# Loads in order of use, products in runs by kind, and scores and comparisons moved in a recurrent attention kernel with a routed block

## The chip, the cores and the metric

One core of one Trainium2 chip runs the kernel. Its engines are TensorE (PE, whose weight loads the profile lists as PEld), VectorE (DVE), ScalarE (ACT), GpSimd (POOL) and SyncE (SP), which issues DMAs here. The metric is the device time of one execution in microseconds (us): the median of the runs.

## What is computed

The first part is a recurrence over 768 steps, for 4 batches of 8 heads of width 48:

```python
for t in range(S):
    cur = np.einsum('bhd,bhe->bhde', u[None] * kt, vt)
    y[:, :, t] = np.einsum('bhd,bhde->bhe', rt, state + cur)
    state = wt[:, :, :, None] * state + np.einsum('bhd,bhe->bhde', kt, vt)
```

The heads are laid side by side to rows `x` of 384. The second part scores each row against `w_gate`, takes in each batch the 128 rows with the highest scores, and adds to these rows what two matrices (384 x 1024 and 1024 x 384, with a relu between) make of them, times the sigmoid of the score. The other rows pass through:

```python
scores = np.einsum('bsd,d->bs', x, w_gate)
for b in range(B):
    top_idx = np.argpartition(-scores[b], capacity)[:capacity]
    xe = x[b, top_idx]
    ye = np.maximum(xe @ w1, 0.0) @ w2
    out[b, top_idx] = xe + g[:, None] * ye
```

## The kernel before, in words

The sequence is cut into 24 chunks of 128 rows, six in each batch, and the recurrence is turned into matrix products within a chunk and a state of 48 x 48 for each head, carried from chunk to chunk. All is float32. Heads stand in pairs, one head in the lower and one in the upper 64 partitions, so that four pairs make tiles of 128 x 512.

One chunk goes through these steps. Four loads bring `w`, `k`, `r` and `v` (L120 to L128), in runs of 48 numbers. `decays_t` (L202) transposes `w` on PE to PSUM. `scans` (L206) multiplies it up from both ends on DVE, two scans of 511 numbers. `scaled` (L239) transposes `k` and `r` on PE and multiplies them with the scans on DVE: K and R. `own_products` (L245) makes r k u on POOL; `own_values` (L251) sums it on DVE ("own") and multiplies `v` with the sum on POOL (`vo`). `scores` (L259) multiplies K and R on PE; `masked` (L269) takes the lower triangle on DVE, in two operations of 512. `back` (L275) transposes K back on PE and copies it on ACT (`kt`). `outputs_t` (L282) makes the chunk's output on PE: for each pair of heads first products of `v` and the masked scores (L290, all 128 rows of the array), then, if there is an old state, products of the state and R (L298, 64 rows each), added in the same PSUM bank. ACT copies the result; `rows_out` (L305) transposes it, adds `vo` on DVE to `x` and stores `x`. `row_scores` (L315) multiplies `x` with `w_gate` and sums, one operation on DVE. `carry_products` (L323) and `carry` (L335) make the new state on PE, DVE and POOL. `range_check` (L230) sums on ACT what of `w` lies out of its range; a general path behind the main one is taken only if there is any.

When all six chunks of a batch have scores, `mixture(b)` (L353) runs: the scores are spread over 128 x 768 by PE transposes and ACT copies (`every`), six DVE operations compare each chunk's scores with all that do not lie ahead of it (L380), 21 small products and two DVE operations make ranks, `pick` marks who has which rank, products make the row numbers, an indirect DMA of POOL gathers the rows (`xe`), PE transposes them, and DVE and ACT make the gate. It is a generator: each `yield` ends a piece. `forward` (L464) is a second one, with eight pieces of hidden products (six matrix products in each, two hidden halves that ACT copies out with a relu) and eight of last products; at its end the rows are scattered back.

The order of the work is written out by hand: `turn(i)` (L528) lists the steps, for chunks i-1 to i+2 at once, and under `manual_schedule` each engine keeps that order. A turn calls `mix` twice, one piece of the mixture each, and `fed` twice, for one and two pieces of the forward (`PIECES` is 3). A mixture starts two turns after its batch's last chunk was begun and takes twelve pieces, six turns. Turns go from -2 to 24; then a tail (L559 to L567) runs the last mixture and the last two forwards.

Buffers set further limits. `w`, `k` and `r` have four each, `v` five. PSUM has eight banks: one for `w`, two for all other transposes and small results (psT), two for the scores, and one each for output (psY), state (psK) and forward (psM). `load(i + 5)` at the end of turn i brings all four inputs of chunk i+5 into the buffers of chunk i+1 (`v`: of chunk i). `load(3)` stands both ahead of the turns (L137) and in turn -2 (L551). Both weight matrices are loaded at the end of turn 0, in two DMAs of 1.5 MB. All of these DMAs, and the stores of `x`, are issued by SP in that order.

Of the kernel before, what the change touches and what calls it, by code (L numbers as in the profile page):

```python
# [38 lines left out]
def kernel(  # L39
# [80 lines left out]
    def load(n):  # L120
        if n >= N:
            return
        b, ci = chunks[n]
        for bufs, x in ((w_bufs, w), (k_bufs, k), (r_bufs, r), (v_bufs, v)):
# [5 lines left out]
    load(0)  # L130
    u_bc = consts.tile([L, H, D], FP32)
    nc.sync.dma_start(out=u_bc, in_=_rows(u, L))
    load(1)
    wg_bc = consts.tile([L, C], FP32)
    nc.sync.dma_start(out=wg_bc, in_=_rows(moe_w_gate, L))
    load(2)
    load(3)  # L137
    w1 = consts.tile([L, NDC, F], FP32)
    w2 = consts.tile([L, NFC, C], FP32)

    def load_weights():
        nc.sync.dma_start(out=w1, in_=moe_w1.rearrange("(n p) f -> p n f", p=L))
        nc.sync.dma_start(out=w2, in_=moe_w2.rearrange("(n p) c -> p n c", p=L))


    ident = consts.tile([L, L], FP32)
# [19 lines left out]
    behind = consts.tile([L, S], FP32)  # L166
    nc.gpsimd.memset(behind[:, L:S], 1.0)
    nc.vector.tensor_copy(out=behind[:, 0:L], in_=before_f)
# [100 lines left out]
    def masked(t):  # L269
        ps = t.pop("ps_s")  # L270
        t["sc"] = lev.tile([L, 2, HP, L], FP32, tag="sc", name="sc")
        for par in (0, 1):
            nc.vector.tensor_mul(t["sc"][:, par], ps[:, par], _heads(before_f, HP))  # L273

    def back(t):  # L275
        ps = transposed(psT, "t", lambda j: t["K"][:, j, :])
# [5 lines left out]
    def outputs_t(t):  # L282

        n = t["n"]
        vt = v_bufs[n % VBUF]
        old = state.get(n)
        ps = psY.tile([L, HP, L], FP32, tag="y", name="ps_yt")
        for j in range(HP):
            for par in (0, 1):
                nc.tensor.matmul(  # L290
                    ps[DP * par:DP * par + DP, j, :], vt[:, 2 * j + par, :],
                    t["sc"][:, par, j, :], start=True, stop=(old is None),
                )
            if old is None:
                continue
            for par in (0, 1):
                rows = slice(DP * par, DP * par + DP)
                nc.tensor.matmul(  # L298
                    ps[DP * par:DP * par + D, j, :], old[rows, j, :], t["R"][rows, j, :],
                    start=False, stop=True,  # L300
                )
        t["yt"] = lev.tile([L, HP, L], FP32, tag="yt", name="yt")
        nc.scalar.copy(out=t["yt"], in_=ps)  # L303
# [11 lines left out]
    def row_scores(t):  # L315
        b, ci = chunks[t["n"]]
        scr = lev.tile([L, C], FP32, tag="scr", name="scr")
        nc.vector.tensor_tensor_reduce(
            out=scr, in0=t.pop("x"), in1=wg_bc, scale=1.0, scalar=0.0, op0=ALU.mult,
            op1=ALU.add, accum_out=score[:, b, ci:ci + 1],  # L320
        )

    def carry_products(t):  # L323
# [26 lines left out]

    groups = [(c0, min(L, CAP - c0)) for c0 in range(0, CAP, L)]

    def mixture(b):  # L353


        every = mod.tile([L, S], FP32, name="every")
        for hf in range(2):
            ps = psT.tile([L, NHF, L], FP32, tag="t", name="ps_e")
            for q in range(NHF):
                c = hf * NHF + q  # L360
                nc.tensor.transpose(  # L361
                    ps[:, q, :], score[:, b, c:c + 1].to_broadcast([L, L]), ident
                )
            nc.scalar.copy(
                out=every[:, hf * NHF * L:(hf + 1) * NHF * L],
                in_=ps.rearrange("p q t -> p (q t)"),
            )
        yield


        ahead = mod.tile([L, NCH, S], BF16, name="ahead")
        won = mod.tile([L, NCH], FP32, name="won", bufs=2)
        for cs in ((0,), (1, 2), range(3, NCH)):
            if 0 not in cs:
                yield
            for c in cs:
                if c >= NCH:
                    continue
                lo = c * L
                nc.vector.scalar_tensor_tensor(  # L380
                    out=ahead[:, c, lo:S], in0=every[:, lo:S], scalar=score[:, b, c:c + 1],
                    in1=behind[:, 0:S - lo], op0=ALU.is_le, op1=ALU.mult,
                    accum_out=won[:, c:c + 1],
                )
            yield
# [12 lines left out]
        for gi, (c0, n) in enumerate(groups):
# [65 lines left out]
    def forward(b, n, rows, where, xe, xeT, gate):  # L464

        hid = mod.tile([L, NFC, L], FP32, name="hid")
        for f0 in range(0, NFC, 4):
            ps = psM.tile([L, 4, L], FP32, tag="m", name="ps_h")
# [25 lines left out]
        yield  # L494
# [73 lines left out]


    def general(gen):  # L570
        u_t = gen.tile([D, H], FP32, name="u_t")
        nc.sync.dma_start(out=u_t, in_=u.rearrange("h d -> d h"))
        for b in range(B):
# [27 lines left out]
            for c in range(NCH):  # L601
                x = lev.tile([L, C], FP32, tag="x", name="x", bufs=3)
                nc.sync.dma_start(out=x, in_=out[b, c * L:(c + 1) * L, :])
                scr = lev.tile([L, C], FP32, tag="scr", name="scr")
                nc.vector.tensor_tensor_reduce(
                    out=scr, in0=x, in1=wg_bc, scale=1.0, scalar=0.0,
                    op0=ALU.mult, op1=ALU.add, accum_out=score[:, b, c:c + 1],
                )
# [41 lines left out]
```

## Time and profile before

| | us |
|---|---|
| median of 3 runs | 272.96 |
| lowest and highest | 271.13, 276.75 |
| the profiled execution | 272.69 |
| its span, first to last instruction | 270.9 |
| PE busy, DVE busy | 230.1, 211.8 |
| POOL busy, ACT busy | 98.9, 77.0 |

The profile shows one execution. Times of rows count from the start of the span. A line of a timeline gives start, duration, engine, line, operation, output and inputs, the number of instructions merged (a matrix product in float32 counts twice) and in brackets how long the engine sat idle before, and what ended that. Ends of matrix products are modelled, so the start of the next instruction is the safer mark. In a row of windows, each engine's busy time (and count) stands in the order PE, PEld, DVE, ACT, POOL, then the granted share of PE's clock, the DMA share and GB/s.

### The profile page before, as it was taken

Reading aid. Unit: us, or ns where it says so; the run is one execution under the profiler, and the core shown is the slowest. Engines: PE = TensorE matmul, PEld = TensorE weight load, DVE = VectorE, ACT = ScalarE, POOL = GpSimd, SP = SyncE. Lnnn points to the kernel's source line nnn. Section 1 sums busy time; section 2 is a strip of 40 time slices with the busy share of each in tenths; the row PEclk is TensorE's granted clock in tenths of the full one; section 3 lists DMA queues with packets and bytes.
Section 4 is the critical chain, followed back from the end, with each engine's and each line's share of the span. In section 5 each row is a group of like instructions: output and inputs, shape, how many; then the busy total and the mean of one; then the engine's idle time right before and its main releaser. Section 6 shows DMA issues by size and latency. Waiting matters only on the chain.

```text
span 270.9 us, 5843 instructions
## 1 busy us (share of the span) xinstructions
PE 230.1 (85%) x2290; PEld 169.9 (63%) x2290; DVE 211.8 (78%) x431; ACT 77.0 (28%) x201; POOL 98.9 (37%) x108
## 2 busy tenths in 40 slices
PE   3783999999798699795999899994999899989780
PEld 2572677776665467674688476584778566685740
DVE  6894478999999998999999999789889994373010
ACT  5450203333442121344323213233213301220100
POOL 3243405554433550844055326334236331102000
PEclk9998569999999858999999999999899999999997
DMA  9999999999996363488545635944000000201001
GB/s 129 180 176 166 162 285 327 179 191 205 193 173 115 67 114 87 92 171 119 111 76 109 127 75 96 171 108 72 31 30 2 29 31 23 68 29 29 31 0 42
DMA packets 109732, 29.96 MB, mean 111 GB/s; under 512 B 104576, under 2 KB 108928, under 8 KB 109696
## 3 DMA queue, kind: packets, MB, share of 16 engines
q1 hardware_dynamic: 109184, 27.93, 58.2%
q0 software_dynamic: 512, 1.57, 1.8%
q8 instruction: 20, 0.33, 0.6%
q14 instruction: 16, 0.13, 0.2%
HBM read 23.99 MB, written 5.51 MB: 109 GB/s over the span
## 4 chain that ended last, share of the span: by engine, by line
PE 44%; DVE 7%; ACT 4%; issue 1%; POOL 0%; ACTq 0%
PE ps_h L471 9%; PE ps_f L481 8%; PE ps_yt L290 6%; PE ps_yt L298 6%; PE ps_t L199 5%; PE ps_s L264 4%; PE ps_kv L330 2%; ACT kt L278 1%; ACT hid L476 1%; PE ps_w L199 1%; DVE left L224 1%; PE ps_e L361 1%; DVE right_buf L212 1%; DVE scr L444 1%; PE ps_y L199 1%
## 5 line engine op out<-in xcount | busy, mean ns | idle before, releaser
L255 POOL TENSOR_TENSOR vo<-v_buf,own 128x384 f32<-128x384 f32 x24 | 25.2, 1051 | 106.5 <-DVE own L253 102.4
L290 PE MATMUL ps_yt<-sc,v_buf 128*64 128x128 f32 x384 | 41.8, 309 | 4.0 <-DVE x L309 4.0
L303 ACT COPY yt<-ps_yt 128x512 f32<-128x512 f32 x24 | 14.1, 586 | 106.9 <-PE ps_yt L298 99.0
L273 DVE TENSOR_TENSOR sc<-ps_s,before_f 128x512 f32<-128x512 f32 x48 | 30.8, 682 | 12.4 <-PE ps_s L264 12.4
L298 PE MATMUL ps_yt<-R,state 64*48 64x128 f32 x320 | 35.7, 302 | 0.0
L290 PEld LDWEIGHTS ps_yt<-sc,v_buf 128*64 128x64 f32 x384 | 20.1, 141 | 21.2 <-issue 14.1
L212 DVE TENSOR_TENSOR_SCAN right_buf<-ps_w,from_right 128x511 f32<-128x511 f32 x24 | 29.0, 1210 | 5.3 <-PE ps_w L199 5.3
L248 POOL TENSOR_TENSOR rk<-r_buf,k_buf 128x384 f32<-128x384 f32 x24 | 30.9, 1289 | 4.0 <-DMA r_buf<-in_r_dram 4.0
L224 DVE TENSOR_TENSOR_SCAN left<-ps_w,from_left 128x511 f32<-128x511 f32 x24 | 30.7, 1280 | 0.9
L264 PE MATMUL ps_s<-R,K 48*128 48x128 f32 x384 | 30.6, 304 | 0.0
L264 PEld LDWEIGHTS ps_s<-R,K 48*128 48x128 f32 x384 | 25.7, 204 | 4.6 <-issue 2.3
L471 PE MATMUL ps_h<-xeT,w 128*128 128x128 f32 x192 | 25.5, 283 | 2.0 <-ACT hid L476 1.4
L380 DVE SCALAR_TENSOR_TENSOR ahead<-every,score,behind 128x768 bf16<-128x768 f32 (+5 forms) x24 | 27.0, 1165 | 0.1
L481 PE MATMUL ps_f<-w,hid 128*128 128x384 f32 x64 | 24.3, 506 | 2.2 <-ACT hid L476 2.2
L249 POOL TENSOR_TENSOR rk<-rk,u_bc 128x384 f32<-128x384 f32 x24 | 25.3, 1053 | 2.6 <-DMA u_bc<-in_u_dram 0.8
L199 PE MATMUL ps_w<-ident,w_buf 128*128 128x128 f32 x96 | 16.5, 301 | 10.1 <-DVE slots L162 4.2
L471 PEld LDWEIGHTS ps_h<-xeT,w 128*128 128x128 f32 x192 | 23.1, 195 | 3.0 <-ACT hid L476 1.8
L298 PEld LDWEIGHTS ps_yt<-R,state 64*48 64x48 f32 x320 | 14.0, 123 | 15.2 <-issue 14.8
L278 ACT COPY kt<-ps_t 128x512 f32<-128x512 f32 x24 | 14.0, 585 | 30.3 <-PE ps_t L199 30.1
L199 PE MATMUL ps_t<-ident,r_buf 128*128 128x128 f32 x96 | 16.5, 298 | 3.7 <-ACT kt L278 2.3
L243 DVE TENSOR_TENSOR R<-ps_t,left 128x512 f32<-128x512 f32 x24 | 16.4, 684 | 3.9 <-PE ps_t L199 2.0
L199 PEld LDWEIGHTS ps_w<-ident,w_buf 128*128 128x128 f32 x96 | 12.7, 157 | 10.7 <-issue 10.7
(89 smaller groups left out, 326.1 us busy)
## 6 DMA issues: line engine op xcount, KB each, us to landing
w_buf<-in_w_dram SPq DMA_DIRECT2D x25, 192.0 KB, 4.1
k_buf<-in_k_dram SPq DMA_DIRECT2D x25, 192.0 KB, 4.8
r_buf<-in_r_dram SPq DMA_DIRECT2D x25, 192.0 KB, 5.0
v_buf<-in_v_dram SPq DMA_DIRECT2D x25, 192.0 KB, 4.3
out_dram<-x SPq DMA_DIRECT2D x24, 192.0 KB, 2.1
w<-in_moe_w_dram SPq DMA_DIRECT2D x2, 1536.0 KB, 9.7
u_bc<-in_u_dram SPq DMA_DIRECT2D x1, 192.0 KB, 4.6
wg_bc<-in_moe_w_gate_dram SPq DMA_DIRECT2D x1, 192.0 KB, 5.2
```

The source lines that it names most:

```text
L199: nc.tensor.transpose(ps[:, j, :], src(j), ident)
L212: nc.vector.tensor_tensor_scan(out=flat[:, W - 2::-1], data0=wt[:, W - 1:0:-1], data1=from_right.rearrange("p j t -> p (j t)")[:, W - 2::- ...
L224: nc.vector.tensor_tensor_scan(out=left.rearrange("p j t -> p (j t)")[:, 1:W], data0=wt[:, 0:W - 1], data1=start.rearrange("p j t -> p (j ...
L248: nc.gpsimd.tensor_mul(rk, r_bufs[n % NBUF][:, :, 0:D], k_bufs[n % NBUF][:, :, 0:D])
L249: nc.gpsimd.tensor_mul(rk, rk, u_bc)
L264: nc.tensor.matmul(ps[:, par, j, :], t["K"][rows, j, :], t["R"][rows, j, :], start=True, stop=True,)
L273: nc.vector.tensor_mul(t["sc"][:, par], ps[:, par], _heads(before_f, HP))
L290: nc.tensor.matmul(ps[DP * par:DP * par + DP, j, :], vt[:, 2 * j + par, :], t["sc"][:, par, j, :], start=True, stop=(old is None),)
L298: nc.tensor.matmul(ps[DP * par:DP * par + D, j, :], old[rows, j, :], t["R"][rows, j, :], start=False, stop=True,)
L380: nc.vector.scalar_tensor_tensor(out=ahead[:, c, lo:S], in0=every[:, lo:S], scalar=score[:, b, c:c + 1], in1=behind[:, 0:S - lo], op0=ALU. ...
L471: nc.tensor.matmul(ps[:, q, :], w1[:, dc, (f0 + q) * L:(f0 + q + 1) * L], xeT[:, dc, :], start=(dc == 0), stop=(dc == NDC - 1),)
L481: nc.tensor.matmul(ps, hid[:, fc, :], w2[:, fc, :], start=(fc == 0), stop=(fc == NFC - 1))
```

## The change

Loads are issued in order of use: `loads(n)` brings `v` of chunk n-2, `k` and `r` of n-1 and `w` of n; each turn i calls `loads(i + 5)`, from turn -1 on. The weights come in seven parts, one a turn from turn 2. The output products run by kind. Both masks are one operation. The score product goes to POOL and its sum to ACT, but for the last chunk. Each chunk is compared with the chunks behind it and with itself two turns after its own, and `mixture` begins with the ranks, in six pieces, and starts one turn later. In the last batch every second half of the hidden products takes the psY bank.

```diff
+    def loads(n):
+        load(v_bufs, v, n - 2)
+        load(k_bufs, k, n - 1)
+        load(r_bufs, r, n - 1)
+        load(w_bufs, w, n)
+    load(w_bufs, w, 0)
+    load(k_bufs, k, 0)
+    load(r_bufs, r, 0)
+    load(w_bufs, w, 1)
     u_bc = consts.tile([L, H, D], FP32)
     nc.sync.dma_start(out=u_bc, in_=_rows(u, L))
+    loads(2)
+    loads(3)
...
+    weights = [
+        (w1[:, i, :], moe_w1[i * L:(i + 1) * L, :]) for i in range(NDC)
+    ] + [
+        (w2[:, i:i + 2, :], moe_w2[i * L:(i + 2) * L, :].rearrange("(n p) c -> p n c", p=L))
+        for i in range(0, NFC, 2)
+    ]
...
     def masked(t):
...
-        for par in (0, 1):
-            nc.vector.tensor_mul(t["sc"][:, par], ps[:, par], _heads(before_f, HP))
+        nc.vector.tensor_mul(
+            t["sc"].rearrange("p q j t -> p (q j) t"), ps.rearrange("p q j t -> p (q j) t"),
+            _heads(before_f, H),
+        )
...
         for j in range(HP):
             for par in (0, 1):
                 nc.tensor.matmul(
                     ps[DP * par:DP * par + DP, j, :], vt[:, 2 * j + par, :],
-                    t["sc"][:, par, j, :], start=True, stop=(old is None),
+                    t["sc"][:, par, j, :], start=(j == 0), stop=(old is None),
+                    skip_group_check=True,
                 )
-            if old is None:
-                continue
+        for j in range(HP if old is not None else 0):
             for par in (0, 1):
...
     def row_scores(t):
...
+        nc.gpsimd.tensor_mul(scr, t.pop("x"), wg_bc)
+        nc.scalar.activation(
+            out=scr, in_=scr, func=AF.Copy, accum_out=score[:, b, ci:ci + 1]
+        )
...
+    def compared_t(t):
...
+        ps = psT.tile([L, L], FP32, tag="t", name="ps_e")
+        nc.tensor.transpose(ps, score[:, b, ci:ci + 1].to_broadcast([L, L]), ident)
+        nc.scalar.copy(out=against[b][0][:, ci * L:(ci + 1) * L], in_=ps)
+    def compared(t):
...
+        if ci > 0:
+            nc.vector.tensor_scalar(
+                out=ahead[:, ci, 0:lo], in0=every[:, 0:lo], scalar1=own, scalar2=None,
+                op0=ALU.is_ge, op1=ALU.add, accum_out=lost[:, ci, 0:1],
+            )
+        nc.vector.scalar_tensor_tensor(
+            out=ahead[:, ci, lo:hi], in0=every[:, lo:hi], scalar=own, in1=after_f,
+            op0=ALU.is_ge, op1=ALU.mult, accum_out=lost[:, ci, 1:2],
+        )
...
+            pool, tag = (psY, "y") if b == B - 1 and f0 % 8 == 4 else (psM, "m")
+            ps = pool.tile([L, 4, L], FP32, tag=tag, name="ps_h")
...
     def turn(i):
+        if 0 <= i - 3 < N and chunks[i - 3][1] == NCH - 1:
+            mixing.append(mixture(chunks[i - 3][0]))
...
         step(rows_out, i - 1)
+        if i == N:
+            row_scores_soon(work[N - 1], work[N - 1]["x"])
+        step(compared_t, i - 2)
         mix()
...
         step(own_values, i + 1)
-        step(row_scores, i - 1)
+        step(compared, i - 2)
+        if i < N:
+            step(row_scores, i - 1)
         mix()
-        load(i + 1 + NBUF)
-        if i == 0:
-            load_weights()
+        if i > -2:
+            loads(i + 5)
+        if i > 1:
+            load_weights(1 if NCH > 2 else 100)
...
+        step(compared_t, N - 1)
+        fed(NFC // 4)
+        step(compared, N - 1)
+        fed(NFC // 4)
         mixing.append(mixture(B - 1))
-        mix()
-        fed(NFC)
-        mix(6)
+        mix(2)
         fed(NFC // 4)
         mix(2)
-        fed(2 * NFC - NFC - NFC // 4)
+        fed(NFC)
         mix(1000)
         fed(1000)
```

`row_scores_soon` is the old score operation on DVE.

## Rows read from the trace of the kernel before

**Rows 1.** Page, part 1: busy time, share of the span, instructions of each engine.

```profile
PE 230.1 (85%) x2290; PEld 169.9 (63%) x2290; DVE 211.8 (78%) x431; ACT 77.0 (28%) x201; POOL 98.9 (37%) x108
```

**Rows 2.** Timeline, DVE, turn 4: start us, us, engine, line, operation, count, idle before.

```profile
49.25 0.53 DVE L253 TENSOR_REDUCE own<-rk 128x8 f32<-128x384 f32 x1
50.65 1.29 DVE L273 TENSOR_TENSOR sc<-ps_s,before_f 128x512 f32<-128x512 f32 x2 [0.40 <-PE ps_s L264]
...
53.18 0.68 DVE L243 TENSOR_TENSOR R<-ps_t,left 128x512 f32<-128x512 f32 x1
...
56.63 0.53 DVE L253 TENSOR_REDUCE own<-rk 128x8 f32<-128x384 f32 x1
```

**Rows 3.** Timeline, PE, a chunk without old state, then turn 20.

```profile
179.87 1.09 PE L290 MATMUL ps_yt<-sc,v_buf 128*64 128x128 f32 x16
...
196.56 1.16 PE L264 MATMUL ps_s<-R,K 48*128 48x128 f32 x16
...
200.65 0.44 PE L290 MATMUL ps_yt<-sc,v_buf 128*64 128x128 f32 x4
...
203.54 0.67 PE L330 MATMUL ps_kv<-v_buf,kt 128*64 128x48 f32 x16
...
205.68 1.16 PE L264 MATMUL ps_s<-R,K 48*128 48x128 f32 x16
```

**Rows 4.** Timeline: links of the new order, from several turns.

```profile
14.08 0.83 POOL L255 TENSOR_TENSOR vo<-v_buf,own 128x384 f32<-128x384 f32 x1 [4.73 <-DVE own L253]
14.87 1.01 POOL L248 TENSOR_TENSOR rk<-r_buf,k_buf 128x384 f32<-128x384 f32 x1
...
49.53 0.62 ACT L234 ACTIVATE junk<-w_buf,low 128x384 f32<-128x384 f32 x1
...
50.27 0.62 ACT L234 ACTIVATE junk<-w_buf,high 128x384 f32<-128x384 f32 x1
...
158.09 0.59 ACT L278 COPY kt<-ps_t 128x512 f32<-128x512 f32 x1 [1.69 <-PE ps_t L199]
...
159.98 0.60 PE L199 MATMUL ps_t<-ident,r_buf 128*128 128x128 f32 x4
...
160.69 0.69 DVE L243 TENSOR_TENSOR R<-ps_t,left 128x512 f32<-128x512 f32 x1 [0.33 <-PE ps_t L199]
```

**Rows 5.** Timeline: compares of DVE beside a POOL product, and alone.

```profile
79.22 1.58 DVE L380 SCALAR_TENSOR_TENSOR ahead<-every,score,behind 128x768 bf16<-128x768 f32 x1
79.95 1.72 POOL L248 TENSOR_TENSOR rk<-r_buf,k_buf 128x384 f32<-128x384 f32 x1
...
237.72 1.02 DVE L380 SCALAR_TENSOR_TENSOR ahead<-every,score,behind 128x768 bf16<-128x768 f32 x1
...
241.09 0.35 DVE L380 SCALAR_TENSOR_TENSOR ahead<-every,score,behind 128x128 bf16<-128x128 f32 x1
```

**Rows 6.** Page, part 6, DMA issues; then the timeline of turn 1.

```profile
w_buf<-in_w_dram SPq DMA_DIRECT2D x25, 192.0 KB, 4.1
...
25.34 1.09 PE L199 MATMUL ps_w<-ident,w_buf 128*128 128x128 f32 x4 [4.15 <-DMA w_buf<-in_w_dram]
...
29.32 0.53 DVE L253 TENSOR_REDUCE own<-rk 128x8 f32<-128x384 f32 x1
```

**Rows 7.** Timeline, PE, a hole in turn 9; then windows: busy, granted clock, DMA.

```profile
93.07 0.69 PE L290 MATMUL ps_yt<-sc,v_buf 128*64 128x128 f32 x4 [2.23 <-DVE x L309]
...
93.00:96.00 3.00, 2.93 (x20) 1.36 (x20) 2.90 (x6) 0.00 (x0) 0.00 (x0) 0.50 0.64 147
```

**Rows 8.** Timeline, DVE, from own in turn 18 to the mask of turn 19.

```profile
183.09 0.53 DVE L253 TENSOR_REDUCE own<-rk 128x8 f32<-128x384 f32 x1
...
187.23 1.28 DVE L273 TENSOR_TENSOR sc<-ps_s,before_f 128x512 f32<-128x512 f32 x2
```

**Rows 9.** Timeline: the last own reduction; a wait within the last forward.

```profile
221.51 0.54 DVE L253 TENSOR_REDUCE own<-rk 128x8 f32<-128x384 f32 x1
...
253.69 1.49 PE L471 MATMUL ps_h<-xeT,w 128*128 128x128 f32 x11 [0.75 <-ACT hid L476]
```

More of the change, by code (lines that the diff above doesn't have):

```diff
@@ L118, with load @@
                 nc.any.memset(bufs[i][:, :, D:DP], value)
[L120 to L124, printed above, removed]
+    def load(bufs, x, n):
+        if n < N:
+            b, ci = chunks[n]
             nc.sync.dma_start(
@@ L128, in load, with load_weights @@
             )
-    load(0)
+    def loads(n):
[7 more added lines that the diff above has]
+    load(w_bufs, w, 1)
     u_bc = consts.tile([L, H, D], FP32)
     nc.sync.dma_start(out=u_bc, in_=_rows(u, L))
-    load(1)
+    loads(2)
+    loads(3)
     wg_bc = consts.tile([L, C], FP32)
     nc.sync.dma_start(out=wg_bc, in_=_rows(moe_w_gate, L))
-    load(2)
-    load(3)
     w1 = consts.tile([L, NDC, F], FP32)
     w2 = consts.tile([L, NFC, C], FP32)
-    def load_weights():
-        nc.sync.dma_start(out=w1, in_=moe_w1.rearrange("(n p) f -> p n f", p=L))
-        nc.sync.dma_start(out=w2, in_=moe_w2.rearrange("(n p) c -> p n c", p=L))
+    weights = [
[4 more added lines that the diff above has]
+    ]
+    def load_weights(n):
+        while n > 0 and weights:
+            to, src = weights.pop(0)
+            nc.sync.dma_start(out=to, in_=src)
+            n -= 1
     ident = consts.tile([L, L], FP32)
@@ L164 @@
     nc.vector.tensor_tensor(out=before_f, in0=col, in1=row, op=ALU.is_lt)
-    behind = consts.tile([L, S], FP32)
-    nc.gpsimd.memset(behind[:, L:S], 1.0)
-    nc.vector.tensor_copy(out=behind[:, 0:L], in_=before_f)
+    after_f = consts.tile([L, L], FP32)
+    nc.vector.tensor_tensor(out=after_f, in0=col, in1=row, op=ALU.is_gt)
     count = setup.tile([L, NCH], INT32)
@@ L299, in outputs_t @@
                     ps[DP * par:DP * par + D, j, :], old[rows, j, :], t["R"][rows, j, :],
-                    start=False, stop=True,
+                    start=False, stop=True, skip_group_check=True,
                 )
@@ L317, in row_scores, with row_scores_soon @@
         scr = lev.tile([L, C], FP32, tag="scr", name="scr")
+        nc.gpsimd.tensor_mul(scr, t.pop("x"), wg_bc)
+        nc.scalar.activation(
+            out=scr, in_=scr, func=AF.Copy, accum_out=score[:, b, ci:ci + 1]
+        )
+    def row_scores_soon(t, x):
+        b, ci = chunks[t["n"]]
+        scr = lev.tile([L, C], FP32, tag="scr", name="scr")
         nc.vector.tensor_tensor_reduce(
-            out=scr, in0=t.pop("x"), in1=wg_bc, scale=1.0, scalar=0.0, op0=ALU.mult,
-            op1=ALU.add, accum_out=score[:, b, ci:ci + 1],
+            out=scr, in0=x, in1=wg_bc, scale=1.0, scalar=0.0, op0=ALU.mult, op1=ALU.add,
+            accum_out=score[:, b, ci:ci + 1],
         )
@@ L351 @@
     groups = [(c0, min(L, CAP - c0)) for c0 in range(0, CAP, L)]
-    def mixture(b):
[L356 to L385, printed above, removed]
@@ new lines @@
+    against = {}
+    def compared_t(t):
+        b, ci = chunks[t["n"]]
+        if ci == 0:
+            against[b] = (
+                mod.tile([L, S], FP32, name="every", bufs=2),
+                mod.tile([L, NCH, S], BF16, name="ahead", bufs=2),
+                mod.tile([L, NCH, 2], FP32, name="lost", bufs=2),
+            )
+            nc.gpsimd.memset(against[b][2][:, 0, 0:1], 0.0)
+        ps = psT.tile([L, L], FP32, tag="t", name="ps_e")
+        nc.tensor.transpose(ps, score[:, b, ci:ci + 1].to_broadcast([L, L]), ident)
+        nc.scalar.copy(out=against[b][0][:, ci * L:(ci + 1) * L], in_=ps)
@@ new lines, in compared @@
+    def compared(t):
+        b, ci = chunks[t["n"]]
+        every, ahead, lost = against[b]
+        own = score[:, b, ci:ci + 1]
+        lo, hi = ci * L, (ci + 1) * L
+        if ci > 0:
[6 more added lines that the diff above has]
+            op0=ALU.is_ge, op1=ALU.mult, accum_out=lost[:, ci, 1:2],
+        )
@@ L386, in mixture @@
+    def mixture(b):
+        every, ahead, lost = against.pop(b)
         ps = psT.tile([L, NCH], FP32, tag="t", name="ps_r")
         for c in range(NCH):
-            for e in range(c + 1):
+            for e in range(c, NCH):
                 nc.tensor.matmul(
                     ps[:, c:c + 1], ahead[:, e, c * L:(c + 1) * L], ones[:, 0:1],
-                    start=(e == 0), stop=(e == c),
+                    start=(e == c), stop=(e == NCH - 1),
                 )
         rank = mod.tile([L, NCH], FP32, name="rank", bufs=2)
-        nc.vector.tensor_sub(rank, behind_n, won)
@@ L395, in mixture @@
-        nc.vector.tensor_add(rank, ps, rank)
+        nc.vector.tensor_add(rank, lost[:, :, 0], lost[:, :, 1])
+        nc.vector.tensor_add(rank, rank, behind_n)
+        nc.vector.tensor_sub(rank, rank, ps)
         yield
@@ L467, in forward @@
         for f0 in range(0, NFC, 4):
-            ps = psM.tile([L, 4, L], FP32, tag="m", name="ps_h")
+            pool, tag = (psY, "y") if b == B - 1 and f0 % 8 == 4 else (psM, "m")
+            ps = pool.tile([L, 4, L], FP32, tag=tag, name="ps_h")
             for q in range(4):
@@ L528, in turn @@
     def turn(i):
-        if i - 2 >= 0 and i - 2 < N and chunks[i - 2][1] == NCH - 1:
-            b = chunks[i - 2][0]
-            mixing.append(mixture(b))
+        if 0 <= i - 3 < N and chunks[i - 3][1] == NCH - 1:
+            mixing.append(mixture(chunks[i - 3][0]))
         step(own_products, i + 1)
@@ L603, in general @@
                 nc.sync.dma_start(out=x, in_=out[b, c * L:(c + 1) * L, :])
[L604 to L608, printed above, removed]
+                t = dict(n=b * NCH + c)
+                row_scores_soon(t, x)
+                compared_t(t)
+                compared(t)
             for _ in mixture(b):
```

## The prediction, made before the change was run

> **What bounds the kernel now.** The table of busy time comes first: PE is busy for 85% of the span, DVE for 78%, no other engine for half of it [rows 1]. Two engines so near to each other mean that stages differ, so next comes the timeline of one turn in each kind of stage, and in it the time from one own reduction (`own`, L253, the last DVE operation of a turn before the score product) to the next. I call its end "own end" and count turns by `i`.
>
> In a turn without the mixture's forward work (turn 4) own end lies at 57.16, that of the turn before at 49.78: 7.38 us. DVE is idle in it for 0.40 only, ahead of the mask [rows 2]. The turn is a ring: PE's score products, then DVE's mask, sum, K and x, then PE's output products, which wait for x, then the next scores. From R's start to own end DVE needs 3.98 (53.18 to 57.16), from the mask's start to R 2.53 [rows 2].
>
> In a turn with forward work (turn 20) PE runs without a hole: scores at 196.56, the next at 205.68, 9.12 us [rows 3]. The output products take 2.89 of it (200.65 to 203.54), since groups of four that use the whole array and groups of four that use half its rows alternate; in a chunk without old state sixteen of the first kind stand in one run and take about 1.0 [rows 3].
>
> So PE bounds the turns with forward work, the ring the others. Turns 1 and 2 are late for another reason: PE waits 4.15 us for a `w` load [rows 6].
>
> **The change part by part.** *Output products in runs by kind.* Sixteen of the first kind take 1.0 [rows 3]; sixteen of the second are not shown in a run. Bounds: nothing gained (2.89), or half a run's time for the second kind, which uses half the array's rows at once (1.5). I take 1.95, twice the run that is shown: PE gives up 0.95 a turn in the 20 turns with a state. A turn with forward work then needs 9.12 - 0.95 + 0.1 (one score transpose a turn) = 8.3 on PE.
>
> *Both masks in one operation.* Compare the same operation at two widths: 1.02 for 768 and 0.35 for 128 [rows 5], so 1.05 ns an element and 0.21 fixed. One fixed part is all that can go: 0 to 0.2 a turn. I take 0, since DVE has slack below.
>
> *Score products on POOL and ACT.* DVE gives up 0.47 a turn (mask start 50.65, less 0.40 idle, less own end) [rows 2]. But look where the work goes. POOL runs in order, and the new product stands behind `vo`, which waits for own; ACT's sum stands behind that product, and ahead of the next turn's copy `kt`; PE's score transpose `ps_e` waits for the score and for a psT buffer; R's transposes stand behind `ps_e` on PE; DVE's R waits for them, and the scans and the next own stand behind R. That is a new ring, once round in a turn:
> own end to `vo` 0.07, `vo` 0.83, product 1.01, with 0.04 between them [rows 4]: 1.95. A compare that holds the port ahead of it 0.1, hand-over to ACT 0.1: 2.15. ACT's sum like one range check, 0.74 from start to start: 2.9. `kt` 0.59: 3.5 [rows 4]. `ps_e` is one transpose of the four that take 0.60, taken as 0.11: 3.6. R's transposes to R 0.71 [rows 4]: 4.3. R to own end 3.98 [rows 2]: **8.3**. A forward piece lies between `ps_e` and R's transposes; two pieces and the state products fill 2.14 [rows 3], so I take 0.7 for one: **9.0** with forward work.
> Bounds of the new prices: POOL product 1.01 to 1.72, what such a product took beside a DVE compare [rows 5]; ACT's sum 0.6 to 0.8.
>
> *Comparisons per chunk.* In turn i chunk i-2 is compared. The strip on the diagonal costs 0.35 alone [rows 5] and must let `vo` finish (0.9 after own end); the strip before it has 128 to 640 elements and one tensor input, so by the line through rows 5 0.35 to 0.88, which fits beside `vo`. Both are done 1.1 after own end. Bounds: 0.5, and 1.6 where each waits for a POOL product. DVE then has 7.38 - 0.40 - 0.47 + 1.1 = 7.6 a turn, less than the ring of 8.3, so it isn't late; PE at 8.3 isn't either.
> The Trainium skill (SBUF — State Buffer, "Who interferes with whom") says that a VectorE operation with two SBUF inputs and a GpSimd one that reads SBUF exclude each other, but that `tensor_scalar` in the form that writes its accumulator can't enter the mode that takes the shared port. By that rule the longer strip leaves `vo` alone and the sum stays at 262; no run here shows such a strip beside POOL, and without the rule the third rival's 282 follows.
>
> *Loads.* Before issues 25 loads of each tensor for 24 chunks: the fourth chunk is loaded twice, the second time in turn -2, and `w` of that chunk is what PE waits for [rows 6]. The new order has 11 loads and `u` ahead of that `w`, where 16 loads and both vectors stood; loads wait for no buffer that the same turn reads, so stores behind them on SP go out sooner. The weights come in seven parts, one a turn from turn 2, before turn 11 needs them. I count the wait of 4.15 as gone (bounds: 0, and 7 with the slow products that follow it).
>
> *Sum.* Own end of turn 1: 29.85 [rows 6] - 4.15 = 25.7. Turns 2 to 7: 6 x 8.3, to 75.5. A mixture is now shorter: rank products (0.7, like a piece), pick (a DVE operation of 768 with two inputs, 1.02 to 1.58 [rows 5]; 1.4, of which 0.9 shows past R) and three transposes (0.5) add 2.1 over three turns; 8 to 10: 27.0, to 102.5. The turn after the gate: before, gate and score product hold the mask until 3.61 after own end [rows 8]; now 1.1 + 3.15 = 4.3, then 2.53 and 3.98: 10.8, for turn 11, to 113.3. Turns 12 to 16: 5 x 9.0 + 2.1, to 160.4. Turn 17: 10.8, to 171.2. Turns 18 to 21: 36.0 + 1.6, to 208.8. Turn 22 has no scans: R at 4.3 + 0.7 + 0.5, then 1.2: to 215.5; before it ends at 222.05 [rows 9]. From there to the end before takes 270.9 - 222.05 = 48.85. Of this the six compares of the last batch (237.72 to 241.44) shrink to one pair, 1.2: -2.5 [rows 5]. The other bank lets the second half of the hidden products start without the wait of 0.75 [rows 9], and I take as much again ahead of the last products: -1.5. So 44.85: the span ends at 260.3. The profiled execution took 272.69 for a span of 270.9, 1.8 around it, and equals the median of 272.96: **262 us**.
>
> So most of what runs and moved scores free isn't seen: before needs 7.4 and 9.1 a turn, after 8.3 and 9.0. The gain comes from the start, the gate turns and the tail.
>
> **The rivals.**
> *The new ring doesn't bind*: product or sum are shorter than I say, or the order on the engines lets the transposes pass. For it: POOL's spans are rough, and in turn 20 of before PE is the later one anyway. Against: each link is in program order on its engine. Then 7.6 and 8.3 a turn: 9 turns (2 to 10) and 9 plain turns with forward work each gain 0.7: 262 - 12.6 = 249 to 250.
> *The clock falls in the turns without forward work.* There R's transposes start 3.6 after own end; these and `w`'s (0.9), the outputs (1.95) and the state products (0.6) end at 7.05, and scores to output transposes take 2.5 (200.65 - 196.56, less a piece and 0.9) [rows 3]. So PE is done with them 1.25 after the next own end and waits for `ps_e` until 3.5: a hole of 2.2 in each of turns 2 to 10. In before a hole of 2.23 ahead of the output products was followed by a granted clock of 0.50, and four products took 0.69 where they take 0.44 [rows 3, 7]. Against: PE is at work in some three quarters of such a turn, and the hole is no longer than that one. At some 2 us each (an estimate: the scores and output products of one turn at half speed, less what the ring hides), three to five of nine make 268 to 272: no change that can be measured.
> *The port, which ends slower.* If every comparison, the long strip too, holds the port against POOL, `vo` starts 0.35 to 0.88 later and the product behind it is held up too, as the product of 1.72 was [rows 5]. I put that at 0.95 a turn; the ring makes it 9.25 and 9.95, in 21 turns (2 to 22): 262 + 20 = 282. From 0.77 a turn on it decides against the change. For it: what a compare and a product do to each other [rows 5]. Against: it needs every strip, since the short one alone costs 0.1.
>
> **How the numbers follow.** My forecast 0.52, no ring 0.20, clock 0.14, port 0.14. A change of 2% (5.5 us, about what a measurement of this kernel tells from none) puts the bounds at 267.5 and 278. The forecast's own range is 254 to 270 (0.2 to 0.4 a turn either way, the bounds of the start), so 0.45 of it is faster, 0.07 within; no ring gives 0.19 and 0.01; clock 0.13 within and 0.01 slower; port 0.02 within and 0.12 slower. Faster 0.64, same 0.23, slower 0.13. The range takes in most of no ring and of clock and leaves out the port: 248 to 277.
>
> **What would show it.** Right: own ends 8.2 to 8.5 apart in turns 2 to 7; PE idle ahead of `ps_e`, put down to ACT; ACT idle ahead of its sum until POOL's product; output products near 1.95; no wait for `w` in turn 1; 24 loads of each tensor. Wrong: own ends 7.6 apart (no ring), `vo` starting 0.4 or more after own end (port), a granted clock near 0.5 in several of turns 2 to 10, or PE still waiting for loads there.

## The result, and the profile after

The changed kernel takes 264.56 us (median of 4 runs, 263.75 to 265.16); the kernel before, run beside it, 274.6 (271.13 to 276.75). The ratio is 0.972, with a 95% interval from 0.965 to 0.980: faster by 2 to 3.5%. The forecast was 262, with a range of 248 to 277 and 0.64 on faster. Medians here are over all executions of a kernel, while ratios leave out those more than 1.5% above its fastest.

In the profiled execution the span is 261.9 us, where 260.3 was forecast. Own ends, by stage:

| end of own in turn | before | predicted | after |
|---|---|---|---|
| 1 | 29.85 | 25.7 | 25.79 |
| 7 | 78.84 | 75.5 | 76.80 |
| 10 | 108.88 | 102.5 | 104.89 |
| 11 (after the gate) | 117.70 | 113.3 | 115.72 |
| 16 | 164.68 | 160.4 | 163.55 |
| 17 (after the gate) | 174.35 | 171.2 | 174.38 |
| 22 | 222.05 | 215.5 | 219.38 |
| end of span | 270.9 | 260.3 | 261.9 |

Lines of the page after: part 1, which answers to [rows 1], then POOL's `vo` (busy time, mean ns), then the loads of `w`, which answer to the first of [rows 6]:

```profile
PE 214.9 (82%) x2290; PEld 175.5 (67%) x2290; DVE 199.3 (76%) x405; ACT 91.8 (35%) x263; POOL 110.6 (42%) x134
...
L270 POOL TENSOR_TENSOR vo<-v_buf,own 128x384 f32<-128x384 f32 x24 | 20.1, 836 | 99.9 <-DVE own L268 95.7
...
w_buf<-in_w_dram SPq DMA_DIRECT2D x24, 192.0 KB, 4.7
```

PE lost 15.2 us of work and DVE 12.5, and the span only 9.0: both engines now stand idle for longer than before. What the engines wait for is in the list of waits (engine, line, what ended the wait: us in total, times, longest):

```profile
ACT scr L337 <- POOL scr L336: 27.9, 18, 2.2
...
PE ps_e L392 <- ACT kt L295: 21.0, 21, 2.5
...
DVE R L258 <- ACT every L393: 9.2, 8, 1.9
```

Read from the bottom, these are the forecast's new ring backwards: DVE's R waits for what follows the score's transpose `ps_e`, the transpose waits for ACT's copy `kt`, and ACT's sum waits for POOL's product. Here is the timeline of turn 4, once round the ring (to be laid beside [rows 2, 4]):

```profile
42.49 0.53 DVE L268 TENSOR_REDUCE own<-rk 128x8 f32<-128x384 f32 x1
...
42.93 0.34 DVE L402 TENSOR_SCALAR_CACHE_REDUCE ahead<-every,score 128x128 bf16<-128x128 f32 x1
...
43.09 0.83 POOL L270 TENSOR_TENSOR vo<-v_buf,own 128x384 f32<-128x384 f32 x1 [4.42 <-DVE own L268]
...
43.20 0.88 DVE L406 SCALAR_TENSOR_TENSOR ahead<-every,score,after_f 128x128 bf16<-128x128 f32 x1
...
43.89 1.05 POOL L336 TENSOR_TENSOR scr<-x,wg_bc 128x384 f32<-128x384 f32 x1
...
44.97 0.52 ACT L337 ACTIVATE scr<-scr 128x384 f32<-128x384 f32 x1 [1.50 <-POOL scr L336]
...
45.49 0.57 ACT L295 COPY kt<-ps_t 128x512 f32<-128x512 f32 x1
...
46.11 0.32 PE L392 MATMUL ps_e<-ident,score 128*128 128x128 f32 x1 [1.55 <-ACT kt L295]
46.47 0.27 ACT L393 COPY every<-ps_e 128x128 f32<-128x128 f32 x1 [0.41 <-PE ps_e L392]
...
46.79 0.66 PE L214 MATMUL ps_t<-ident,r_buf 128*128 128x128 f32 x4 [0.36 <-ACT every L393]
...
47.54 0.69 DVE L258 TENSOR_TENSOR R<-ps_t,left 128x512 f32<-128x512 f32 x1 [0.99 <-ACT every L393]
...
51.00 0.53 DVE L268 TENSOR_REDUCE own<-rk 128x8 f32<-128x384 f32 x1
```

From own end 43.02 to own end 51.53 it is 8.51 us, and each link starts within 0.1 us of the end of the one before. Turn 5 takes 8.81, and one link in it is another: ACT's sum is over early enough, and `kt` waits for PE's transposes of K, which the slow output products of turn 4 (47.81 to 51.46) have pushed back. Turn 3 is like it.

```profile
53.51 0.51 ACT L337 ACTIVATE scr<-scr 128x384 f32<-128x384 f32 x1
...
54.29 0.59 ACT L295 COPY kt<-ps_t 128x512 f32<-128x512 f32 x1 [0.18 <-PE ps_t L214]
```

Turn 13, with forward work, takes 8.60. The output products there, in runs by kind, start at 129.22 and end where the state products start, at 131.25: 2.03, where 1.95 was taken and 2.89 was shown before [rows 3].

```profile
129.22 1.09 PE L308 MATMUL ps_yt<-sc,v_buf 128*64 128x128 f32 x16
130.25 1.08 PE L316 MATMUL ps_yt<-R,state 64*48 64x128 f32 x16
131.25 0.67 PE L356 MATMUL ps_kv<-v_buf,kt 128*64 128x48 f32 x16
```

### The profile page after: what moved, and what is told of

The parts are those of the page before. It is cut to its first block, busy times and chain, and to the rows that moved or that the text cites. A ratio compares the mean times of both kernels' runs of the same rounds, so it can differ in the third digit from the quotient of the medians.

```text
span 261.9 us, 5911 instructions
## 1 busy us (share of the span) xinstructions
PE 214.9 (82%) x2290; PEld 175.5 (67%) x2290; DVE 199.3 (76%) x405; ACT 91.8 (35%) x263; POOL 110.6 (42%) x134
## 5 line engine op out<-in xcount | busy, mean ns | idle before, releaser
L270 POOL TENSOR_TENSOR vo<-v_buf,own 128x384 f32<-128x384 f32 x24 | 20.1, 836 | 99.9 <-DVE own L268 95.7
L287 DVE TENSOR_TENSOR sc<-ps_s,before_f 128x1024 f32<-128x1024 f32 x24 | 29.2, 1218 | 6.3 <-PE ps_s L279 6.3
L308 PE MATMUL ps_yt<-sc,v_buf 128*64 128x128 f32 x384 | 30.2, 307 | 2.6 <-DVE x L327 2.6
L308 PEld LDWEIGHTS ps_yt<-sc,v_buf 128*64 128x64 f32 x384 | 23.8, 153 | 7.3 <-DVE x L327 3.3
L263 POOL TENSOR_TENSOR rk<-r_buf,k_buf 128x384 f32<-128x384 f32 x24 | 24.7, 1029 | 4.5 <-DMA r_buf<-in_r_dram 4.5
L336 POOL TENSOR_TENSOR scr<-x,wg_bc 128x384 f32<-128x384 f32 x23 | 26.0, 1129 | 0.0
L392 PE MATMUL ps_e<-ident,score 128*128 128x128 f32 x24 | 7.7, 323 | 21.0 <-ACT kt L295 21.0
L316 PE MATMUL ps_yt<-R,state 64*48 64x128 f32 x320 | 23.9, 294 | 0.0
L337 ACT ACTIVATE scr<-scr 128x384 f32<-128x384 f32 x23 | 12.0, 523 | 28.0 <-POOL scr L336 27.9
L316 PEld LDWEIGHTS ps_yt<-R,state 64*48 64x48 f32 x320 | 18.4, 130 | 4.0 <-issue 3.9
```

Source lines behind the costliest of these rows:

```text
L263: nc.gpsimd.tensor_mul(rk, r_bufs[n % NBUF][:, :, 0:D], k_bufs[n % NBUF][:, :, 0:D])
L270: nc.gpsimd.tensor_mul(t["vo"], v_bufs[t["n"] % VBUF][:, :, 0:D], o.to_broadcast([L, H, D]))
L287: nc.vector.tensor_mul(t["sc"].rearrange("p q j t -> p (q j) t"), ps.rearrange("p q j t -> p (q j) t"), _heads(before_f, H),)
L308: nc.tensor.matmul(ps[DP * par:DP * par + DP, j, :], vt[:, 2 * j + par, :], t["sc"][:, par, j, :], start=(j == 0), stop=(old is None), ski ...
L316: nc.tensor.matmul(ps[DP * par:DP * par + D, j, :], old[rows, j, :], t["R"][rows, j, :], start=False, stop=True, skip_group_check=True,)
L336: nc.gpsimd.tensor_mul(scr, t.pop("x"), wg_bc)
```

## The experiments

All ratios are to the kernel before, run on the same chip (medians 274.05, 274.08 and 272.89 in the three sets). My theory was the forecast's: the ring through POOL's product sets the turns. The rivals were that DVE with its comparisons sets them, or PE at its lowered clock.

**The product out of the ring.** On POOL the score product stands right behind `x`, so ahead of the next `vo`; ACT's sum stays where it was.

```diff
         nc.gpsimd.tensor_mul(scr, t.pop("x"), wg_bc)
+        t["scr"] = scr
+
+    def row_sums(t):
+        b, ci = chunks[t["n"]]
+        scr = t.pop("scr")
         nc.scalar.activation(
...
             row_scores_soon(work[N - 1], work[N - 1]["x"])
+        else:
+            step(row_scores, i - 1)
         step(compared_t, i - 2)
...
         if i < N:
-            step(row_scores, i - 1)
+            step(row_sums, i - 1)
```

> The changed kernel with POOL's score product issued right behind x, ahead of vo; ACT's sum keeps its place. Ring theory (own, vo, product, sum, kt, ps_e, R's transposes, R, scans, own sets the turn): product and sum leave the ring, own ends come 7.5 to 7.9 apart in turns 4 to 7 and 8.2 to 8.4 in turns 12 and 13, the time falls to 251 to 257. Rival 1 (DVE's comparisons set the turn): own ends stay at 8.5, time 263 to 266. Rival 2 (PE with its lowered clock sets the turn): turns 4 to 7 stay at 8.5, 12 and 13 stay at 8.6.

Measured: 250.13 us (249.17 to 251.03), ratio 0.920 (0.907 to 0.933): 14.4 less than the change as it stands, from one instruction's place, and a little less than I expected. In the timeline of turn 5 the sum on ACT stands behind nothing but ACT's own work, and the product runs while DVE does the scans:

```profile
47.07 0.51 ACT L342 ACTIVATE scr<-scr 128x384 f32<-128x384 f32 x1
...
47.85 0.58 ACT L295 COPY kt<-ps_t 128x512 f32<-128x512 f32 x1 [0.18 <-PE ps_t L214]
...
50.88 1.00 POOL L336 TENSOR_TENSOR scr<-x,wg_bc 128x384 f32<-128x384 f32 x1 [0.57 <-DMA r_buf<-in_r_dram]
```

That turn takes 7.43 and turn 13 7.67, where the forecast's first rival (no ring) had 7.6 and 8.3, and its 249 to 250 us is what was measured. Both rivals had the turns stay at 8.5, so neither holds. The granted clock is 1.00 in turns 4 and 5 here, so the low clock went with the ring; what it had cost is told under the clock below.

**The other end of the ring.** The score's transpose goes behind R's and `w`'s transposes:

```diff
-        step(compared_t, i - 2)
         mix()
         fed(PIECES // 2)
         step(scaled, i + 1, "R", r_bufs, "left")
         step(decays_t, i + 2)
+        step(compared_t, i - 2)
```

> The changed kernel with ps_e behind R's and w's transposes on PE; product, sum and kt as they are. Ring theory: the link from ps_e and its copy to R's transposes is cut, these wait for K's product or for kt only; own ends 7.7 to 8.2 apart in turns 4 to 7 and about 8.4 in 12 and 13, time 256 to 262. If POOL and ACT alone were the ring, without ps_e: no difference, 263 to 266.

Measured: 253.65 us (252.75 to 256.02), ratio 0.934 (0.918 to 0.949). That is better than I expected. The ring is shorter, not gone: in turn 5 (7.83 us) R's transposes still wait for `kt`, which stands behind ACT's sum, but no longer for `ps_e` and its copy.

```profile
50.07 0.52 ACT L337 ACTIVATE scr<-scr 128x384 f32<-128x384 f32 x1 [1.39 <-POOL scr L336]
...
50.59 0.57 ACT L295 COPY kt<-ps_t 128x512 f32<-128x512 f32 x1
...
51.21 0.66 PE L214 MATMUL ps_t<-ident,r_buf 128*128 128x128 f32 x4 [1.45 <-ACT kt L295]
...
52.14 0.27 PE L392 MATMUL ps_e<-ident,score 128*128 128x128 f32 x1
```

**Both cuts together.**

> The changed kernel with both cuts: the score product right behind x on POOL, and ps_e behind R's and w's transposes. Ring theory: either cut alone already brings the turn to DVE's work (7.4) or PE's, so both together give little more: own ends 7.4 to 7.6 apart in turns 4 to 7, time 246 to 251. If the cuts added up (10 and 14 us): 240.

Measured: 243.91 us (241.27 to 244.64), ratio 0.890 (0.883 to 0.898), better than I expected and the fastest of all. Against the first cut alone, turns 4 and 5 stay (7.43 and 7.42), while turn 3 goes from 7.19 to 6.62, turn 14 from 10.87 to 10.09 and turn 16 from 9.69 to 9.13. The windows of turns 3 and 4 (columns as in [rows 7]; the third pair is DVE) show what bounds them now: DVE is busy for 6.51 of 6.62 and for 7.33 of 7.43.

```profile
32.71:39.33 6.62, 6.38 (x89) 5.45 (x85) 6.51 (x13) 3.34 (x11) 4.26 (x5) 1.00 0.96 196
39.33:46.76 7.43, 6.85 (x90) 5.60 (x87) 7.33 (x15) 3.53 (x11) 4.33 (x5) 1.00 1.10 247
```

**The score back on DVE, in the same place** (behind the comparisons), which takes POOL and ACT's sum out of the ring and adds half a microsecond to DVE:

```diff
-        if i < N:
-            step(row_scores, i - 1)
+        if i < N and i >= 1:
+            row_scores_soon(work[i - 1], work[i - 1]["x"])
```

> The changed kernel with product and sum of the score back in one DVE operation, in the same place. Ring theory: the way over POOL and ACT is gone, DVE needs 0.5 more a turn: own ends 7.9 to 8.2 apart in turns 4 to 7, 8.3 to 8.6 in 12 and 13, time 255 to 261, so faster than the changed kernel although DVE has more to do. Rival 1 (DVE sets the turn): 0.5 a turn slower, 272 to 277. Rival 2 (PE): no difference, 263 to 266.

Measured: 265.53 us (262.65 to 266.99), ratio 0.968 (0.949 to 0.988): no gain over the change. The expectation was wrong; the time is the one that I had given for PE as the bound. The timeline of turn 5 says why:

```profile
51.32 1.06 POOL L263 TENSOR_TENSOR rk<-r_buf,k_buf 128x384 f32<-128x384 f32 x1
51.44 1.35 DVE L344 CUSTOM_DVE_ANT_0 scr<-x,wg_bc 128x384 f32<-128x384 f32 x1
...
52.72 1.21 DVE L287 TENSOR_TENSOR sc<-ps_s,before_f 128x1024 f32<-128x1024 f32 x1
```

I had priced the score by the 0.47 it took ahead of the mask in the kernel before. Behind the comparisons it falls beside POOL's `rk` and takes 1.28 (51.44 to 52.72), ending 0.3 us after `rk` does. DVE becomes the bound (busy for 8.61 of the 8.71 us of turn 5): one bound was exchanged for another of the same length. PE is not that bound, since in turn 4 it is busy for 6.63 of 8.69, where DVE is busy for 8.59:

```profile
41.76:50.45 8.69, 6.63 (x61) 5.28 (x63) 8.59 (x17) 1.46 (x5) 3.54 (x4) 0.80 0.84 174
```

So this run alone speaks neither for the ring nor against it, and the next one does what it was meant to do.

**The score on DVE, ahead of the comparisons:**

```diff
+        if i < N and i >= 1:
+            row_scores_soon(work[i - 1], work[i - 1]["x"])
         step(compared, i - 2)
-        if i < N:
-            step(row_scores, i - 1)
```

> The changed kernel with the score in one DVE operation as in the run with the score on DVE, but ahead of the comparisons, when POOL still waits for own. Theory: there the operation took 1.28 because it met POOL's product and shared its port; here it takes 0.55 and the comparisons still end beside vo: own ends 7.8 to 8.1 apart in turns 4 to 7, time 253 to 259. If DVE's amount of work and not the port made that run slow: 263 to 267 again.

Measured: 255.13 us (254.91 to 258.37) in three of the four executions, ratio 0.939 (0.929 to 0.949). The fourth took 397 and is left out; what held it isn't known. The time is as expected. Three lines of turn 5: the score takes 0.47 up to the comparison, and only `vo` pays a little (1.08 where it takes 0.83).

```profile
48.78 0.55 DVE L344 CUSTOM_DVE_ANT_0 scr<-x,wg_bc 128x384 f32<-128x384 f32 x1
48.94 1.08 POOL L270 TENSOR_TENSOR vo<-v_buf,own 128x384 f32<-128x384 f32 x1 [4.03 <-DVE own L268]
49.25 0.47 DVE L402 TENSOR_SCALAR_CACHE_REDUCE ahead<-every,score 128x256 bf16<-128x256 f32 x1
```

**The same with the late transpose:**

> The changed kernel with the score on DVE ahead of the comparisons and the score's transpose behind R and the decays. If in the kernel with the score ahead of the comparisons DVE bounds the turns without forward work (7.67 with no idle time), the later transpose helps only turns with forward work: 251 to 256 us. Rival: there too R waited for the transposes, so that the cut is worth what it was behind the early product (6 us): 248 to 251. Either way over 244, since DVE carries 0.5 a turn more than in the kernel with both cuts.

Measured: 253.88 us (249.95 to 255.51), ratio 0.924 (0.908 to 0.941), as the first case says; turns 3 to 5 stay at 7.67 to 7.68, with DVE busy for 7.57 to 7.58 of each. With the ring open at both ends, POOL and ACT are the better place for the score: a ratio of 0.890 (0.883 to 0.898) against 0.924. The idea of the move was right, its place in the order wasn't.

**The changed kernel without runs** (output products alternate again, all else as changed):

```diff
-                    start=(j == 0), stop=(old is None),
-                    skip_group_check=True,
+                    start=True, stop=(old is None),
...
-        for j in range(HP if old is not None else 0):
+            if old is None:
+                continue
```

> The changed kernel with the output products in turn again, not in runs. Ring theory: PE needs 0.95 more in the 20 turns with a state, which the waits ahead of ps_e hide in turns 2 to 10 (own ends stay 8.4 to 8.9 apart); turns with forward work go to 9.1 to 9.4, time 269 to 274. Rival 2 (PE sets every turn): 0.95 in 20 turns, 281 to 285.

Measured: 272.1 us (269.83 to 274.31, 10 runs), ratio 0.998 (0.993 to 1.003). So the runs are worth 7.5 us in the changed kernel, where the forecast had most of that hidden. In turns 2 to 5 they are hidden: 8.48 to 8.53 without them, 8.46 to 8.81 with. From turn 12 to 22, with forward work, the kernel loses 4.7 us without them (108.35 against 103.66), but not in every turn: nothing in 13, 17 and 19, 0.3 in 12, 15, 18 and 21, and 0.85 in 14, 16, 20 and 22. In turn 8, the first with mixture work, it loses 3.9: that turn takes 12.94 at a granted 0.76, PE busy for 12.38 of it, where the changed kernel takes 9.03 at 0.81. Turn 10 gives 0.85 of this back (8.86 for 9.71). How much of the 3.9 us is the runs' own work and how much where the lowered clock happens to fall, this run doesn't tell. The windows of turns 7 to 9, and of 13 and 14, without runs:

```profile
68.06:76.58 8.52, 5.45 (x37) 2.75 (x35) 7.42 (x16) 1.35 (x4) 3.79 (x4) 0.77 0.85 162
76.58:89.52 12.94, 12.38 (x136) 9.21 (x136) 7.99 (x18) 4.08 (x13) 4.36 (x6) 0.76 0.53 114
89.52:98.87 9.35, 7.58 (x95) 5.40 (x95) 8.34 (x15) 3.33 (x11) 6.18 (x6) 1.00 0.67 157
...
127.53:136.14 8.61, 7.42 (x85) 5.42 (x84) 7.41 (x15) 1.94 (x5) 3.81 (x4) 1.00 0.74 120
136.14:147.86 11.72, 10.44 (x117) 7.21 (x117) 7.90 (x18) 4.08 (x13) 4.35 (x6) 1.00 0.59 94
```

**Parts alone, on the kernel before.** First the runs only, then the loads and weights only (with the first loads, `loads` and the list of weights of the change):

```diff
-                    t["sc"][:, par, j, :], start=True, stop=(old is None),
+                    t["sc"][:, par, j, :], start=(j == 0), stop=(old is None),
+                    skip_group_check=True,
                 )
-            if old is None:
-                continue
+        for j in range(HP if old is not None else 0):
```

```diff
-        load(i + 1 + NBUF)
-        if i == 0:
-            load_weights()
+        if i > -2:
+            loads(i + 5)
+        if i > 1:
+            load_weights(1 if NCH > 2 else 100)
```

> The kernel before with the output products in runs by kind and nothing else. No ring over POOL here: PE gives up 0.95 in a turn, which shows only where PE sets the turn and DVE has room: 0.4 in turns 4 and 5 (DVE is busy 6.9 of 7.4), 0.5 to 0.9 in turns 14, 16, 17, 20 and 23, nothing in turns 9, 15 and 21, where DVE is full with comparisons. 4 to 8 us in all, ratio 0.97 to 0.985. If runs gave their full 0.95 in 20 turns: 19 us, ratio 0.93.

> The kernel before with the new order of loads (24 of each, weights in seven parts) and nothing else. PE's wait of 4.15 for w in turn 1 goes, and part of the slow products behind it: own end of turn 3 moves from 49.8 to 41 to 45; 4 to 8 us in all, ratio 0.97 to 0.985. Rival (loads are hidden anyway): same time.

Measured: runs 264.91 us (262.73 to 266.68), ratio 0.968 (0.958 to 0.979), 9.2 less; loads 263.67 (262.42 to 266.2), ratio 0.965 (0.956 to 0.974), 10.4 less. Both more than expected. With runs a turn without forward work goes from 7.38 to 6.90 (0.4 less was expected), and DVE is then busy for 6.79 to 6.80 of it. Turn 2 alone brings 3.1: it takes 9.17 at a granted 0.91 instead of 12.27 at 0.66. With the loads, two turns change most: windows of turns 1 and 2 before, then with the new loads.

```profile
19.90:29.85 9.95, 5.56 (x36) 2.88 (x34) 6.41 (x13) 0.57 (x1) 2.79 (x3) 0.74 1.19 164
29.85:42.12 12.27, 12.27 (x114) 9.23 (x110) 7.07 (x14) 3.12 (x9) 3.54 (x4) 0.66 1.19 257
```

```profile
19.51:26.91 7.40, 7.16 (x88) 5.16 (x86) 6.41 (x12) 1.96 (x6) 2.80 (x3) 1.00 1.35 170
26.91:34.28 7.37, 7.13 (x90) 5.13 (x88) 6.88 (x14) 2.57 (x8) 3.52 (x4) 1.00 1.13 200
```

Before, PE waits in turn 1, does only part of that turn's work in it, and then works through turn 2 at a granted 0.66 (PE is busy for all of its 12.27). Without the wait the clock stays at 1.00, and turn 2 takes 7.37. By the end of turn 3 that is 8.1 us (49.78 against 41.65), twice the wait itself. With the runs in place it is 6.7 (45.86 with the runs only, 39.12 with both parts, in the next experiment).

**Runs and loads together, scores and comparisons as before:**

> The kernel before with two parts of the change, the runs by kind and the new order of the loads; scores, masks, comparisons and mixture stay as before. If the two parts add as they stood alone (9.2 and 10.4 us): 252 to 257 us, own ends 6.9 apart in turns 2 to 7, and then the part that moves scores and comparisons costs the change 8 to 12 us, what the ring takes and more. Rival: the two parts cover each other (both free PE in the turns behind the stall): 258 to 262, and the moved scores cost 3 to 6.

Measured: 258.19 us (256.1 to 258.43), ratio 0.948 (0.942 to 0.955): 14.7 less than before by the medians, where the parts add to 19.6, so the number fell to the rival's side. In the ratios it is 5.2% where the parts add to 6.7%, which is still within their intervals. The spans of the profiled executions, one of each kernel, add nearly (before 270.9; runs -9.4, loads -7.9, both -16.6). So whether the two parts overlap stays open. What is clear: this kernel, with two of the parts, is 6.4 us faster than the whole change. Its turns 2 to 5 take 6.90, and DVE is busy for 6.80 of that:

```profile
32.22:39.12 6.90, 6.35 (x85) 5.34 (x86) 6.80 (x14) 2.57 (x8) 3.50 (x4) 1.00 0.85 194
```

So the rest of the change, which is the moved scores and comparisons with the single mask operation and the second bank, costs 12.8 us in its order up to the last own end (206.56 against 219.38) and gives back 5.2 in the tail (47.7 against 42.5). The mask and the bank were not run by themselves.

## Why the prediction was right

**The new ring: right, and shown.** Own ends lie 8.46 to 8.81 apart in turns 2 to 5, with 8.3 forecast. Two cuts at its two ends shorten the kernel by 14.4 and 10.9 us. The links of turn 4 differ from the forecast's to both sides. From own end to ACT's sum it is 1.95 (43.02 to 44.97), where the 2.15 of the forecast had 0.1 each for a comparison ahead of `vo` and for the hand-over to ACT. ACT's sum was taken at 0.74 and takes 0.52 to the start of `kt`. And a link was missing: R's transposes wait, in turns without forward work, not only in order behind `ps_e` but for ACT's copy of it (`every`); from `ps_e` to R's transposes it is 0.68 (46.11 to 46.79), where 0.11 stood in the sum. Turns 3 and 5 close the ring through PE's transposes of K instead of the sum, which the forecast didn't have.

**The ring with forward work: too long.** 9.0 was forecast, 8.6 measured in turns 12, 13, 18 and 19. The forward piece (127.59 to 128.15 in turn 13) runs while ACT copies `every`, so it adds little to the wait that was missing above: from `ps_e` to R's transposes it is 0.83 with the piece (127.43 to 128.26) and 0.68 without. The piece itself takes 0.56, not 0.7. The turns with a mixture piece as well are longer than the sum had them (turn 14: 10.87, turn 15: 10.05), and together turns 12 to 16 take 47.8 against 47.1.

**Runs: right on PE, wrong on the path.** The products take 2.03 instead of 2.89, as taken. That most of what runs and moved scores free isn't seen holds for turns 2 to 5 and, with forward work, for the plain turns 13 and 19 (8.61 without runs, 8.60 and 8.61 with). In the whole kernel runs are worth 7.5 us. The step that failed is that all turns with forward work were added up from one plain turn, in which a ring of 9.0 stood against PE's 8.3: the turns in which mixture work is added do show the runs (turn 14 loses 0.85 without them, 11.72 against 10.87), and so does turn 8 with its 3.9.

**The start: right at turn 1 (25.79 for 25.7), and worth more than was said.** The slow products of turn 2, which the forecast named only in the bound of 7, go too. Its sum had this gain without naming it, since it counted turn 2 as a turn of the ring (8.3) where the kernel before takes 12.27.

**"The gain comes from the start, the gate turns and the tail": the gate turns don't belong there.** Turn 11 takes 10.83, as forecast (10.8), but turns 12 to 17 take 58.7 where they took 56.7 before; the forecast's own sum had 57.9. From the own end of turn 3 to that of turn 22 the changed kernel needs 176.4 us and the one before 172.3. All that it gains is 6.8 by the end of turn 3 and 6.3 in the tail.

**The tail: 42.5, with 44.85 forecast.** From the last `x` to the row numbers (`idx`) it shrank by 2.4 (11.1 to 8.8; 2.5 forecast), from there to the end by 1.9 (1.5 forecast). Before, then after:

```profile
234.02 0.56 DVE L309 TENSOR_TENSOR x<-ps_y,vo 128x384 f32<-128x384 f32 x1 [4.42 <-issue]
...
245.14 0.22 DVE L418 TENSOR_SCALAR idx<-ps_i 128x1 uint32<-128x1 f32 x1 [0.71 <-PE ps_i L412]
```

```profile
229.27 0.56 DVE L327 TENSOR_TENSOR x<-ps_y,vo 128x384 f32<-128x384 f32 x1 [2.92 <-issue]
...
238.03 0.22 DVE L447 TENSOR_SCALAR idx<-ps_i 128x1 uint32<-128x1 f32 x1 [0.40 <-PE ps_i L441]
```

A third gain wasn't counted: from the last own end to the last `x` it is 9.9 instead of 12.0. The outputs run by kind there (2.03 for 2.89); with the runs alone on the kernel before it is 10.3, so there they bring 1.7 of such a 2.1. That no piece of last products (1.56 before) stands ahead of the last scores may be the rest; no run shows it by itself. Errors of 3.8 too short in turns 2 to 22, 0.1 too short in the start and 2.3 too long in the tail leave the 1.6 between 260.3 and 261.9. So the total is better than its terms, and in part that is luck.

**The port: wrong, and the rows say why.** `vo` starts 0.07 to 0.09 after own end in every turn but the last (0.30) and takes 836 ns on average in 24, beside strips of 128 to 640 elements. The other comparison, with two tensor inputs, does wait: in turn 4 it is issued at 43.20 and takes 0.88 for 128 elements that take 0.35 alone [rows 5]; it ends just after `vo` (43.92). That the strips leave `vo` alone agrees with what the Trainium skill (SBUF — State Buffer, "Who interferes with whom") says of `tensor_scalar` in the form that writes its accumulator, on which 262 instead of 282 hung.

**The clock: real, and nearly free.** The rival said that a hole of 2.2 in each of turns 2 to 10 would lower the clock. PE's hole ahead of `ps_e` is 1.55 in turn 4 and 0.24 in turn 5, and the granted share is lower in every second turn. Windows of turns 2 to 5 after:

```profile
25.79:34.25 8.46, 6.47 (x57) 5.15 (x59) 6.43 (x11) 1.76 (x7) 4.25 (x6) 0.80 1.21 206
34.25:43.02 8.77, 8.18 (x117) 6.88 (x115) 6.71 (x13) 4.92 (x15) 4.26 (x5) 1.00 0.92 193
43.02:51.53 8.51, 6.60 (x57) 5.36 (x57) 7.41 (x15) 1.81 (x6) 4.26 (x5) 0.80 1.01 189
51.53:60.34 8.81, 8.21 (x106) 6.97 (x107) 7.49 (x15) 4.88 (x15) 4.27 (x5) 1.00 0.65 140
```

The turns at 0.80 are the shorter ones; those behind them are 0.3 longer. That, not 2, is the price: in turn 4 the output products take 3.65 at the lower clock (47.81 to 51.46) instead of 2.03, and all but 0.3 of it is slack that PE has within the ring; the 0.3 is the later `kt` of turn 5. With both cuts the granted share is 1.00 in turns 3 and 4.

## What to carry to other kernels

When an operation moves to an engine with room, follow each queue it enters: what it stands behind there, what stands behind it, and whether the two close into a ring with the engine it left. Here the busy shares spoke for the move (POOL 37%, ACT 28% before) and its place in POOL's order, behind `vo` instead of ahead of it, cost 14 us. A wait of PE early in a kernel should be priced with the slow clock behind it: here the wait was 4.15 us and its removal brought 8 in the kernel before.

## What was unexpected of the hardware

- Sixteen small float32 products (32 in the profile, which counts each twice) in two runs by kind take 2.03 us; alternating two by two they take 2.89.
- DVE's product-and-sum of 384 takes 0.47 to 0.55 us alone and 1.28 to 1.35 where it is issued while a POOL product runs; that product takes 1.06, and the next one 1.20. Which of the two it is follows from half a microsecond in DVE's order.
- One turn of light PE work (6.5 of 8.5 us busy, holes of over 1.5 us) and one at full clock alternate in turns 2 to 5 (0.80, 1.00, 0.80, 1.00), without a change in the program.
